# Two chunks of queries and probabilities turned by DMA under a rewritten instruction list, in a sorted-attention kernel with a cosine-gated layer behind it

## The chip, the cores and the metric

The kernel runs on one core of one Trainium2 chip. A core has a matrix engine (TensorE, "PE" in the profile, its weight loads "PEld"), a vector engine (VectorE, "DVE"), an engine for functions of one element (ScalarE, "ACT"), a general engine (GpSimd, "POOL") and SyncE ("SP"), which here does nothing but issue DMAs. Each engine works through its own instructions in order and waits on semaphores for the others. 16 DMA engines move data; GpSimd and SyncE each feed a queue of their own to them. The metric is device time in microseconds (us) of one execution, the median of several.

## The reference

Four batches of eight heads, 768 positions, 64 dimensions. The positions form eight blocks of 96. A softmax-like matrix P of 8 by 8 per head, normalised five times by rows and columns, mixes the blocks of keys and of values; each block of queries then attends to one mixed block. The result, 3072 tokens of 512, goes through a layer with a cosine gate.

```python
for _ in range(5):
    P = P - np.max(P, axis=-1, keepdims=True)
    P = np.exp(P)
    P = P / (np.sum(P, axis=-1, keepdims=True) + 1e-09)
    P = P / (np.sum(P, axis=-2, keepdims=True) + 1e-09)
k_sorted = np.einsum('bhij,bhjcd->bhicd', P, k_b).reshape(B, H, S, D)
v_sorted = np.einsum('bhij,bhjcd->bhicd', P, v_b).reshape(B, H, S, D)
scores = scale * np.matmul(q_b, k_sb.transpose(0, 1, 2, 4, 3))
scores = scores - np.max(scores, axis=-1, keepdims=True)
attn = np.exp(scores)
attn = attn / (np.sum(attn, axis=-1, keepdims=True) + 1e-09)
x = np.matmul(attn, v_sb)          # then heads side by side: 3072 x 512
h = x @ w_in
out = (h * np.cos(h)) @ w_out
```

## The kernel before

**Chunks and units.** The tokens are cut into eight chunks `n` of 384 (half a batch each), a chunk into four units `u` of one block. A unit needs its scores (queries against mixed keys, L438 or L745), the row maximum and its subtraction on DVE, the exponent on ACT (`expo`, L515), the probabilities turned (`pT`), the attention product (L570), its normalisation on DVE and that result turned again (`xT`). A chunk then goes up (`up`, L614; chunk 0 in quarters, `up_four`, L798), through sine with a shift on ACT and the gate on DVE, and down (`down`, L639; `down_four`, L819).

**Turning.** A tile is turned either by PE (a matmul with the identity, then a copy out of PSUM by ACT or DVE) or by a DMA transpose that SyncE issues. `expo(n, u, True)` leaves the probabilities to PE (`p_ps` and `p_ev`); without `True` it issues the DMA (L533), which reads one of three `p_buf` tiles in turn. Queries of chunks below `NQ = 3` are loaded by one DMA (L119) and turned by PE (`q_products`, L268, with `q_place_half`); later ones come by eight smaller DMAs (L129) between columns that `zeros_between` has cleared, and SyncE turns them (`q_transpose_dma`, L149). `q_turned` has two halves by the parity of the chunk, `q_mem` and part of `kbuf` hold the untransposed queries.

**Keys and values.** Batches 0 and 1 share one mixing matrix in the places where 128 rows are used, batches 2 and 3 (`g = 1`) another. Batch 0's keys are mixed by `kp` (L408), batch 1's by `ks`, those of batches 2 and 3 by `k_sort_g` from the tile `pair`. `k_swap` moves mixed keys between partition halves by two DMAs (L421, L422). Values arrive in `vbuf`; GpSimd's `v_permute` (L179) copies them to `vperm` in pieces of some value dimensions, and the value products (L726 for batch 0, L448 for batch 1, L458 for batches 2 and 3) read one dimension `d` each as a stationary tile. They take 128 columns from column `d * 96` on, of which 96 belong to `d` and 32 to the next dimension, so the last product of a piece also reads the start of the next piece.

**Order.** There is no scheduler: the order of the calls in the program is the order on every engine. Up to chunk 1's start the list is written out call by call, with extra matmuls on a zero tile (`keep_warm`, the argument `fill`) in places; from `up(1, 0)` on it is in loops with slots. A tile taken from a pool (`big` has three buffers in PSUM, `acc` two) waits until the tile that held the buffer before has been read. GpSimd's queue is also a list: its loads go out between its copies and fills, and a `hold` (a copy of one element, L541, or L426 for `hold_keys`) keeps what is behind it back until a DMA has landed. A load of GpSimd's also waits until the eighth one before it has landed.

Of the kernel before, what the change touches and what calls it, by code (L numbers as in the profile page):

```python
# [18 lines left out]
def kernel(  # L19
# [15 lines left out]
    nc = tc.nc  # L35
# [131 lines left out]
    VQ = 16  # L167
# [58 lines left out]
    def ones(g):  # L226
        nc.gpsimd.memset(vS[g][:, :, D:D + 1], 1.0)
# [196 lines left out]
    def hold_keys():  # L424

        nc.gpsimd.tensor_copy(held[:], kT[1][:, 1, 0, :1])  # L426

    def keys_of(n, u, h2, hp):
        g, b2, ih = where(n)
        z = slice(hp, hp + 2)  # L430
# [7 lines left out]
        nc.tensor.matmul(  # L438
            out, q_of(n, hp)[:, x:x + 128], keys_of(n, u, h2, hp), start=True, stop=True)
# [14 lines left out]

    def v_sort_g(d0, nd, eng, pool, tag):
        ps = pool.tile([128, nd, 4 * NB], FP32, name="vs", tag=tag)
        for t in range(nd):
            nc.tensor.matmul(  # L458
                ps[:, t], v_cols(d0 + t, True), bds[1].rearrange("p x i -> p (x i)"),
                start=True, stop=True)  # L460
        copy_on(eng, vS[1][:, :, d0:d0 + nd], ps[:blk].rearrange("p t n -> p n t"))

# [47 lines left out]
    def expo(n, u, on_pe=False):  # L510
        p = p_bufs[cnt[0] % NP]
        cnt[0] += 1


        nc.scalar.activation(  # L515
            p[:, :, :blk], s_t.pop((n, u)).rearrange("p e h c -> p (e h) c"), AF.Exp,
            scale=scale)
        if u == 0 and n in (NQ, NQ + 1):

            w = 2 * H2 * blk  # L520
            c = 2 * (QZ + D) + (n - NQ) * w
# [197 lines left out]
    def v0(z, pool, tag, fill=0):  # L719
        o = ps["v", z] = pool.tile([128, 8, 2 * NB], FP32, name="vs", tag=tag)  # L720
        keep_warm(fill, o.rearrange("p t n -> p (t n)"))
        for t in range(8):

            d = z * 8 + t
            w = 1 if d >= VN else min(8 - t, 2)
            nc.tensor.matmul(  # L726
                o[:, t:t + w].rearrange("p w n -> p (w n)"), v_cols(d, d >= VN),
                bdv[:, :H].rearrange("p x i -> p (x i)").unsqueeze(1).to_broadcast(
                    [128, w, 2 * NB]), start=True, stop=True)

# [111 lines left out]
        v_sort_g(next(wz), 8, eng, *B)  # L842
        next(wz)

    kp(2, *B)
    kp(0, *B)
# [4 lines left out]
    k_place(2, A, 1)  # L851
    k_place(2, V, 0)
    kp(1, *B)
    k_place(0, A, 0)
    blocks.append(block([pick[:, :, z * PB:(z + 1) * PB] for z in (1, 0)]))
    k_place(1, V, 0)
    k_place(1, A, 1)
    values_matrix()
    k_place(0, A, 1)
    s_ps(0, 0, fill=3)  # L860
    v0(4, *C)
    s_max(0, 0)
    v0(0, *B)
    v0e(4, A)
    s_sub(0, 0)
    s_ps(0, 3)
    v0e(0, A)
    v0(5, *C)
    s_max(0, 3)
    load_w_out(0)  # L870
    v0e(5, A)
    s_ps(0, 1)
    load_w_out(1)
    load_w_out(2)
    load_w_out(3)
    v0(6, *C)
    ones(0)
    expo(0, 0, True)
    s_ps(0, 2)
    s_sub(0, 3)  # L880
    v0(1, *C)
    v0e(6, A)
    s_max(0, 1)
    expo(0, 3, True)
    v0(3, *B, fill=2)
    s_sub(0, 1)
    v0e(1, A)
    p_ps(0, 0, *C, fill=2)
    v0e(3, A)
    s_max(0, 2)  # L890
    v0(7, *C)
    expo(0, 1, True)
    kxp(2)
    v0(2, *B, fill=1)
    p_ev(0, 0, V)
    v0e(7, A)
    s_sub(0, 2)
    kxp(0)
    p_ps(0, 1, *C)
    v0e(2, A)  # L900
    p_ps(0, 3, *C)
    p_ev(0, 1, V)
    expo(0, 2, True)
    kxp(1)
    av_products(0, 0)
    z_turned(1)
    av_norm(0, 0, True)
    av_products(0, 1)
    p_ev(0, 3, A)
    p_ps(0, 2, *C)  # L910
    av_norm(0, 1, True)
    x_ps(0, 0, *B)
    load(kbuf, 0, kin_d[1])
    p_ev(0, 2, A)
    load(vbuf, 64, vin_d[1])
    picks(pick_pair, (2, 3))
    av_products(0, 3, fill=2)
    av_norm(0, 3, True)
    x_ps(0, 1, *C)
    x_ev(0, 0, A)  # L920
    av_products(0, 2)
    q_products(1, 0, 0, 16, *C)
    x_ev(0, 1, A)
    av_norm(0, 2, True)
    x_ps(0, 3, *B)
    q_place_half(1, 0, 1, A)
    up_four(0, 0, 0)
    z_vperm()
    up_four(0, 0, 1)
    x_ev(0, 3, V)  # L930
    q_place_half(1, 0, 0, V)
    up_four(0, 3, 0)
    up_four(0, 3, 1)
    z_turned(0)
    cos_four(0, 0)
    p_pads()
    up_four(0, 1, 0)
    cos_four(0, 3)
    gate_four(0, 0)
    x_ps(0, 2, *C)  # L940
    up_four(0, 1, 1)
    gate_four(0, 3)
    up_four(0, 2, 0)
    cos_four(0, 1)
    up_four(0, 2, 1)
    x_ev(0, 2, V)
    gate_four(0, 1)
    up_four(1, 2, 0)
    cos_four(0, 2)
    up_four(1, 2, 1)  # L950
    gate_four(0, 2)
    up_four(1, 1, 0)
    cos_four(1, 2)
    up_four(1, 1, 1)
    gate_four(1, 2)
    up_four(1, 3, 0)
    cos_four(1, 1)
    up_four(1, 3, 1)
    gate_four(1, 1)
    q_products(1, 1, 0, 16, *C)  # L960
    cos_four(1, 3)
    last = block([pick_pair[:]], *C)
    q_place_half(1, 1, 0, V)
    up_four(1, 0, 0)
    q_place_half(1, 1, 1, A)
    gate_four(1, 3)
    up_four(1, 0, 1)
    s_ps(1, 1)
    spread(bds[1], last)
    cos_four(1, 0)  # L970
    s_ps(1, 0)
    s_max(1, 1)
    down_four(0, 0)
    gate_four(1, 0)
    load_q(2)
    down_four(0, 1)
    load_pair(pair, kin_d, 0 * CD // 2, 1 * CD // 2)
    load_pair(pair, kin_d, 1 * CD // 2, 2 * CD // 2)
    v_permute(slice(64, 128))
    down_four(0, 2)  # L980
    s_sub(1, 1)
    down_four(1, 0)
    s_max(1, 0)
    expo(1, 1, True)
    ks(5, *B)
    s_ps(1, 3)
    s_sub(1, 0)
    kse(5, A)
    down_four(0, 3)
    s_max(1, 3)  # L990
    expo(1, 0, True)
    ks(4, *B)
    s_ps(1, 2)
    down_four(1, 1)
    down_out(0, A)
    s_max(1, 2)
    kse(4, A)
    p_ps(1, 1, *C)
    s_sub(1, 3)
    down_four(1, 2)  # L1000
    p_ev(1, 1, A)
    down_four(1, 3)
    s_sub(1, 2)
    expo(1, 3, True)
    p_ps(1, 0, *B)
    down_out(1, A)
    av_products(1, 1)
    p_ps(1, 3, *B)
    p_ev(1, 0, A)
    av_norm(1, 1, True)  # L1010
    down_four(2, 0)
    expo(1, 2, True)
    p_ev(1, 3, V)
    av_products(1, 0)
    x_ps(1, 1, *B)
    down_four(2, 1)
    av_norm(1, 0, True)
    x_ev(1, 1, A)
    p_ps(1, 2, *B)
    av_products(1, 3)  # L1020
    p_ev(1, 2, A)
    down_four(2, 2)
    av_norm(1, 3, True)
# [179 lines left out]
```

## Time and profile before

| | us |
|---|---|
| median of 3 executions | 235.54 (234.93 to 236.42) |
| profiled execution, its own time | 235.54 |
| its span in the profile | 233.6 |
| PE busy | 224.1 |
| DVE busy | 171.0 |
| ACT busy | 154.4 |
| GpSimd busy | 95.9 |

Times in the profile count from the start of the span, to which the time of an execution adds 1.9 us around it. A row of a timeline reads: start, duration, engine, line of the program, operation, written tile and read tiles, how many instructions were merged; in brackets how long the engine stood idle before and who released it. A duration of PE includes the way through the array, so the distance from one group's start to the next is what a group costs. A row of a stretch ("66.00:70.00") gives its length, the busy time of PE, PEld, DVE, ACT and POOL with their numbers of instructions, PE's granted clock, the share of the 16 DMA engines (several packets at once can take it over 1) and GB/s.

### The profile page before, as it was taken

Reading aid. Unit: us, or ns where it says so; the run is one execution under the profiler, and the core shown is the slowest. Engines: PE = TensorE matmul, PEld = TensorE weight load, DVE = VectorE, ACT = ScalarE, POOL = GpSimd, SP = SyncE. Lnnn points to the kernel's source line nnn. Section 1 sums busy time; section 2 is a strip of 40 time slices with the busy share of each in tenths; the row PEclk is TensorE's granted clock in tenths of the full one; section 3 lists DMA queues with packets and bytes.
Section 4 is the critical chain, followed back from the end, with each engine's and each line's share of the span. In section 5 each row is a group of like instructions: output and inputs, shape, how many; then the busy total and the mean of one; then the engine's idle time right before and its main releaser. Section 6 shows DMA issues by size and latency. Waiting matters only on the chain.

```text
span 233.6 us, 5420 instructions
## 1 busy us (share of the span) xinstructions
PE 224.1 (96%) x2212; PEld 141.8 (61%) x2212; DVE 171.0 (73%) x291; ACT 154.4 (66%) x209; POOL 95.9 (41%) x121
## 2 busy tenths in 40 slices
PE   8778999999999999998999999999999999999994
PEld 3367899567665656655666546655665566556553
DVE  6769867987789867885498885997699769745700
ACT  5648886776889758795788565655665566816621
POOL 7999999399950093992609002600000000000000
PEclk9999999999999999999999999999999999999999
DMA  5999999993999799898999679934933360351012
GB/s 73 227 190 206 203 206 227 204 223 124 124 134 175 123 166 151 130 198 134 139 145 101 96 99 195 170 65 88 177 128 64 73 186 0 68 144 45 3 45 90
DMA packets 67672, 31.19 MB, mean 134 GB/s; under 512 B 56384, under 2 KB 63168, under 8 KB 67392
## 3 DMA queue, kind: packets, MB, share of 16 engines
q0 software_dynamic: 24048, 13.64, 43.3%
q1 hardware_dynamic: 43312, 17.02, 35.1%
q8 instruction: 17, 0.28, 0.5%
q10 hardware_dynamic: 288, 0.20, 0.3%
q14 instruction: 7, 0.06, 0.1%
HBM read 27.27 MB, written 6.29 MB: 144 GB/s over the span
## 4 chain that ended last, share of the span: by engine, by line
PE 82%; DMA 8%; DVE 3%; POOL 3%; ACT 1%; issue 1%; SPq 0%; ACTq 0%; DVEq 0%; POOLq 0%
PE h L614 30%; PE o L639 27%; DMA kv<-in_v_dram 5%; PE h L798 5%; PE o L819 4%; PE sc L438 4%; PE av L570 3%; POOL vperm L179 3%; DMA pT<-p_buf 2%; PE ks L408 2%; PE o L1167 2%; DMA kTs<-kTs 1%; DVE xn L583 1%; PE vs L458 1%; PE pps L776 1%
## 5 line engine op out<-in xcount | busy, mean ns | idle before, releaser
L614 PE MATMUL h<-xT,w_in_t 128*128 128x384 bf16 x448 | 78.4, 326 | 0.0
L639 PE MATMUL o<-w_out_t,gg 128*128 128x512 bf16 x320 | 76.3, 379 | 0.0
L622 DVE TENSOR_TENSOR gg<-c,h 128x768 bf16<-128x768 f32 x56 | 52.7, 949 | 19.5 <-ACT c L618 19.4
L618 ACT ACTIVATE c<-h,half_pi 128x768 f32<-128x768 f32 x56 | 50.4, 900 | 24.5 <-PE h L614 23.6
L614 PEld LDWEIGHTS <-w_in_t 128*128 128x128 bf16 x448 | 42.2, 98 | 26.3 <-DVE xT L259 0.3
L639 PEld LDWEIGHTS <-gg 128*128 128x128 bf16 x320 | 29.1, 99 | 27.8
L515 ACT ACTIVATE p_buf<-s 96x768 bf16<-96x768 f32 x32 | 26.7, 842 | 5.6 <-DVE s L489 4.7
L179 POOL COPY vperm<-kv 64x768 bf16<-64x768 bf16 (+2 forms) x12 | 28.4, 2408 | 4.4 <-DMA kv<-in_v_dram 4.4
L489 DVE TENSOR_TENSOR s<-sc,mx 96x384 f32<-96x384 f32 (+1 forms) x33 | 24.3, 736 | 1.6
L487 DVE TENSOR_REDUCE mx<-sc 96x4 f32<-96x384 f32 (+1 forms) x33 | 24.0, 728 | 0.0
L583 DVE TENSOR_TENSOR xn<-av,r 96x512 bf16<-96x512 f32 x32 | 22.0, 687 | 1.1
L129 POOL DMA_DIRECT2D kv<-in_q_dram x24 | 16.0, 677 | 0.8 <-issue 0.5
L438 PE MATMUL sc<-kTs,q_turned 128*128 128x96 bf16 x224 | 15.4, 206 | 0.3 <-DMA kTs<-kTs 0.3
L257 ACT CAST kTs<-ks 128x512 bf16<-128x512 f32 x20 | 11.3, 582 | 6.3 <-PE ks L408 5.3
L581 DVE RECIPROCAL r<-av 96x8 f32<-96x8 f32 x32 | 6.4, 199 | 12.0 <-PE av L570 11.8
L438 PEld LDWEIGHTS <-q_turned 128*128 128x128 bf16 x224 | 12.6, 98 | 4.0 <-DVE s L489 0.6
L257 ACT COPY kv<-o 128x512 f32<-128x512 f32 (+2 forms) x10 | 5.2, 523 | 14.1 <-PE o L639 11.5
L129 POOL DMA_DIRECT2D q_mem<-in_q_dram x16 | 10.7, 690 | 4.6 <-DMA kv<-in_v_dram 4.2
L819 PE MATMUL o<-w_out_t,gg 128*128 128x512 bf16 x48 | 11.7, 379 | 0.0
L259 DVE COPY kv<-o 128x512 f32<-128x512 f32 (+1 forms) x5 | 3.1, 611 | 11.1 <-PE o L1167 8.5
L798 PE MATMUL h<-xT,w_in_t 128*128 128x192 bf16 x128 | 11.1, 246 | 0.0
L798 PEld LDWEIGHTS <-w_in_t 128*128 128x128 bf16 x128 | 10.5, 98 | 0.0
(128 smaller groups left out, 276.9 us busy)
## 6 DMA issues: line engine op xcount, KB each, us to landing
out_dram<-kv SPq DMA_DIRECT2D x12, 256.0 KB, 2.6
out_dram<-o_s SPq DMA_DIRECT2D x10, 256.0 KB, 3.7
w_in_t<-in_moe_w_in_dram POOLq DMA_DIRECT2D x4, 512.0 KB, 11.6
w_out_t<-in_moe_w_out_dram POOLq DMA_DIRECT2D x4, 512.0 KB, 12.6
kv<-in_k_dram POOLq DMA_DIRECT2D x2, 768.0 KB, 10.0
kv<-in_v_dram POOLq DMA_DIRECT2D x2, 768.0 KB, 13.3
pair<-in_k_dram POOLq DMA_DIRECT2D x2, 768.0 KB, 12.3
kv<-in_v_dram POOLq DMA_DIRECT2D x6, 256.0 KB, 5.6
```

The source lines that it names most:

```text
L129: nc.gpsimd.dma_start(out=q_heads[:, i, :, e], in_=src[:, ih * IC + i, :, e])
L179: nc.gpsimd.tensor_copy(dst, src)
L438: nc.tensor.matmul(out, q_of(n, hp)[:, x:x + 128], keys_of(n, u, h2, hp), start=True, stop=True)
L487: nc.vector.reduce_max(mx[:], scv, axis=AX.X)
L489: nc.vector.tensor_tensor(s, scv, mx.to_broadcast(list(s.shape)), op=ALU.subtract)
L515: nc.scalar.activation(p[:, :, :blk], s_t.pop((n, u)).rearrange("p e h c -> p (e h) c"), AF.Exp, scale=scale)
L583: nc.vector.tensor_tensor(xn.rearrange("p h e d -> p e h d"), avv[:, :, :, :D], r.to_broadcast([blk, 2, H2, D]), op=ALU.mult)
L614: nc.tensor.matmul(h[:, f2, :w], w_in_t[:, kk, f * 128:(f + 1) * 128], xT[n][:, kk], start=(kk == 0), stop=(kk == KC - 1))
L618: nc.scalar.activation(c[:], h[:, :, :w], AF.Sin, bias=half_pi[:, 0:1])
L622: nc.vector.tensor_tensor(gt[n, fp // 2][:, f:f + 2], c[:], h[:, :, :w], op=ALU.mult)
L639: nc.tensor.matmul(o[:], gt[n, f // 4][:, f % 4, ts * 128:(ts + 1) * 128], w_out_t[:, f, :], start=(f == 0), stop=(f == FC - 1))
L798: nc.tensor.matmul(o[:, part, f2 * w:(f2 + 1) * w], w_in_t[:, kk, f * 128:(f + 1) * 128], xT[0][:, kk, h * w:(h + 1) * w], start=(kk == 0) ...
```

## The change

Five things are changed.

1. `NQ` is 2. Chunk 2's queries are no longer loaded by one DMA and turned by 32 transposes of PE and four copies of DVE: `q_mem` is cleared between the heads (`zeros_between(2)`), eight DMAs fill it, and SyncE turns it with two DMA transposes. The fills of `q_turned[0]` (`z_turned(0)`) and the second clearing of `q_mem` before chunk 4 go. Unit 0 of chunks 3 and 4 keeps its place in `kbuf`.
2. Units 1 and 0 of chunk 1 are turned by a DMA transpose (`expo(1, 1)` and `expo(1, 0)` without `True`); eight transposes of PE and a copy go for each.
3. The keys of batches 2 and 3 come to `pair` in four pieces in place of two halves: the last piece before the queries, the other three between GpSimd's copies of batch 1's values.
4. `hold_keys` goes, and the first three of the six value loads of batches 2 and 3, which stood behind it, join the other three. All six now stand behind chunk 4's query loads.
5. The last value product of each block of products takes 96 columns, and writes 96 rows, in place of 128.

The list up to `up(1, 0)` is written anew around this: value and key products, exponents and evictions of chunk 0 in another order and on other engines, the quarters of `up_four` and `down_four` in another order (the down projection of chunk 0's first 128 tokens last), `k_swap` ahead of the last pieces, twelve fills in place of ten.

```diff
-    QR, NQ = 4, 3
+    QR, NQ = 4, 2
...
-    def v_cols(d, permuted):
-        return vperm[:, d * blk:d * blk + 128] if permuted else vv[:, d]
+    def v_cols(d, permuted, m=128):
+        return vperm[:, d * blk:d * blk + m] if permuted else vv[:, d]
...
+            m = 128 if t < nd - 1 else blk
             nc.tensor.matmul(
-                ps[:, t], v_cols(d0 + t, b == 1 or d0 + t >= D // 2)[rows],
+                ps[:m, t], v_cols(d0 + t, b == 1 or d0 + t >= D // 2, m)[rows],
...
+    load_pair(pair, kin_d, 3 * CD // 4, 4 * CD // 4)
+    load_q(2)
...
+    for z in range(4):
+        if z < 3:
+            load_pair(pair, kin_d, z * CD // 4, (z + 1) * CD // 4)
+        v_permute(slice(64, 128), z * VQ, hi=(z + 1) * VQ)
...
-    expo(1, 1, True)
+    expo(1, 1)
...
+    q_transpose_dma(2)
...
-    hold_keys()
-    load_pair(vbuf, vin_d, 0 * CD // 6, 1 * CD // 6)
-    load_pair(vbuf, vin_d, 1 * CD // 6, 2 * CD // 6)
-    load_pair(vbuf, vin_d, 2 * CD // 6, 3 * CD // 6)
...
-    for z in range(3, 6):
+    load_q(4)
+    for z in range(6):
         load_pair(vbuf, vin_d, z * CD // 6, (z + 1) * CD // 6)
-    load_q(4)
```

On GpSimd, from the clearing of `p_buf`'s last tile to the copies of batch 1's values, there stood before (a line, an operation, written and read tile, the shape, how often):

```order
L685 MEMSET p_buf_109 96x8x32
L119 DMA q_mem<-in_q_dram 96x8x256
L92 DMA pair<-in_k_dram 128x3072 x2
L179 COPY vperm<-kv 64x1536 x4
L137 MEMSET kv 96x16x64 x2
```

and at the same place now:

```order
L683 MEMSET p_buf_109 96x8x32
L137 MEMSET q_mem 96x16x64 x2
L92 DMA pair<-in_k_dram 128x1536
L129 DMA q_mem<-in_q_dram 96x4x64 x8
L92 DMA pair<-in_k_dram 128x1536
L179 COPY vperm<-kv 64x1536
L92 DMA pair<-in_k_dram 128x1536
L179 COPY vperm<-kv 64x1536
L92 DMA pair<-in_k_dram 128x1536
L179 COPY vperm<-kv 64x1536 x2
L137 MEMSET kv 96x16x64 x2
```

The one query load has become two fills and eight loads, and the copies alternate with key loads.

Further on GpSimd, from chunk 3's query loads to the copies of the values of batches 2 and 3 (`-` before, `+` now):

```order
 L129 DMA kv<-in_q_dram 96x4x64 x8
-L426 CAST held<-kTs 128x1
-L92 DMA kv<-in_v_dram 128x1024 x3
-L137 MEMSET q_mem 96x16x64 x2
-L541 CAST held<-pT 96x1
-L92 DMA kv<-in_v_dram 128x1024 x3
+L539 CAST held<-pT 96x1
 L129 DMA q_mem<-in_q_dram 96x4x64 x8
+L92 DMA kv<-in_v_dram 128x1024 x6
 L179 COPY vperm<-kv 128x1536 x4
```

All value loads have moved behind the hold on unit (2, 2)'s probabilities and behind chunk 4's queries.

In SyncE's queue, from the load of the mixing weights to the transposes of chunk 3's queries (`q_turned_94` is the half for even chunks, `q_turned_95` the one for odd ones):

```order
 L81 DMA P<-in_sort_net_dram 32x64
-L629 DMA out_dram<-o_s 128x512 x2
-L629 DMA out_dram<-c 128x512
+L531 DMA_TRANSPOSE pT<-p_buf_108 128x8x96
+L627 DMA out_dram<-o_s 128x512
+L531 DMA_TRANSPOSE pT<-p_buf_107 128x8x96
+L149 DMA_TRANSPOSE q_turned_94<-q_mem 128x16x96 x2
+L627 DMA out_dram<-c 128x512
 L421 DMA kTs<-kTs 64x1536
 L422 DMA kTs<-kTs 64x1536
+L627 DMA out_dram<-o_s 128x512
 L149 DMA_TRANSPOSE q_turned_95<-kv 128x16x96 x2
```

Two transposes of probabilities and two of queries now stand ahead of the swap of keys, and one output store behind it.

More of the change, by code (lines that the diff above doesn't have):

```diff
@@ L843, in w_two @@
         next(wz)
-    kp(2, *B)
-    kp(0, *B)
+    kp(2, *B, fill=1)
+    blocks.append(block([pick[:, :, z * PB:(z + 1) * PB] for z in (1, 0)]))
     v_permute(slice(0, 64), 32, False, 8, 40)
@@ L850 @@
     v_permute(slice(0, 64), 56, False, 8, 64)
-    k_place(2, A, 1)
-    k_place(2, V, 0)
+    k_place(2, A, 0)
+    k_place(2, V, 1)
     kp(1, *B)
+    values_matrix()
+    kp(0, *B)
+    k_place(1, V, 0)
+    v0(0, *C)
     k_place(0, A, 0)
[L855 to L858, printed above, removed]
+    k_place(1, V, 1)
+    s_ps(0, 0)
+    v0e(0, A)
+    s_max(0, 0)
+    v0(4, *C, fill=1)
     k_place(0, A, 1)
-    s_ps(0, 0, fill=3)
@@ L861 @@
-    v0(4, *C)
-    s_max(0, 0)
-    v0(0, *B)
+    v0(5, *C)
     v0e(4, A)
+    s_ps(0, 3)
     s_sub(0, 0)
[L866 to L869, printed above, removed]
+    v0e(5, A)
+    v0(2, *C)
     load_w_out(0)
-    v0e(5, A)
-    s_ps(0, 1)
     load_w_out(1)
     load_w_out(2)
+    s_max(0, 3)
     load_w_out(3)
+    expo(0, 0, True)
+    ones(0)
     v0(6, *C)
-    ones(0)
-    expo(0, 0, True)
-    s_ps(0, 2)
+    v0e(2, A)
     s_sub(0, 3)
-    v0(1, *C)
-    v0e(6, A)
-    s_max(0, 1)
@@ L906 @@
+    v0(3, *C, fill=1)
+    s_sub(0, 1)
+    v0e(7, A)
+    s_ps(0, 2, fill=1)
+    v0e(3, A)
+    p_ev(0, 0, V)
+    v0(1, *C)
+    kxp(0)
+    expo(0, 1, True)
+    s_max(0, 2)
+    v0e(1, A)
+    p_ps(0, 1, *B, fill=2)
+    kxp(1)
+    s_sub(0, 2)
+    p_ev(0, 1, A)
+    av_products(0, 0, fill=1)
+    kxp(2)
     z_turned(1)
     av_norm(0, 0, True)
+    p_ps(0, 3, *C, fill=3)
+    expo(0, 2, True)
     av_products(0, 1)
-    p_ev(0, 3, A)
-    p_ps(0, 2, *C)
     av_norm(0, 1, True)
     x_ps(0, 0, *B)
+    p_ev(0, 3, A)
@@ L940 @@
-    x_ps(0, 2, *C)
+    x_ev(0, 2, V)
     up_four(0, 1, 1)
     gate_four(0, 3)
-    up_four(0, 2, 0)
+    up_four(1, 3, 0)
     cos_four(0, 1)
-    up_four(0, 2, 1)
-    x_ev(0, 2, V)
+    up_four(1, 3, 1)
     gate_four(0, 1)
+    up_four(1, 1, 0)
+    cos_four(1, 3)
+    up_four(1, 1, 1)
+    gate_four(1, 3)
+    up_four(1, 0, 0)
+    cos_four(1, 1)
+    up_four(1, 0, 1)
+    gate_four(1, 1)
+    q_products(1, 0, 0, 16, *C)
+    zeros_between(2)
+    cos_four(1, 0)
+    load_pair(pair, kin_d, 3 * CD // 4, 4 * CD // 4)
@@ L948 @@
+    load_q(2)
+    last = block([pick_pair[:]], *C)
+    q_place_half(1, 0, 0, V)
     up_four(1, 2, 0)
-    cos_four(0, 2)
+    q_place_half(1, 0, 1, A)
+    gate_four(1, 0)
     up_four(1, 2, 1)
[L951 to L963, printed above, removed]
@@ new lines @@
+    s_sub(1, 1)
+    down_four(1, 2)
+    s_max(1, 2)
+    expo(1, 1)
+    ks(5, *B)
+    s_ps(1, 0)
+    s_sub(1, 2)
+    kse(5, A)
+    down_four(1, 3)
+    s_max(1, 0)
+    expo(1, 2, True)
+    ks(2, *B)
+    s_ps(1, 3)
+    down_four(2, 1)
+    kse(2, A)
+    s_sub(1, 0)
+    down_out(1, A)
+    down_four(2, 2)
+    s_max(1, 3)
+    expo(1, 0)
+    ks(4, *B)
+    p_ps(1, 2, *B)
+    s_sub(1, 3)
+    kse(4, A)
+    down_four(2, 3)
+    q_transpose_dma(2)
+    p_ev(1, 2, V)
+    expo(1, 3, True)
@@ L976 @@
+    ks(1, *B)
+    ks(3, *C)
+    kse(1, V)
+    av_products(1, 1)
+    down_out(2, A)
+    p_ps(1, 3, *B)
+    av_norm(1, 1, True)
+    av_products(1, 2)
+    p_ev(1, 3, A)
+    down_four(0, 0)
+    av_norm(1, 2, True)
+    kse(3, A)
+    av_products(1, 3)
+    av_products(1, 0)
+    av_norm(1, 0, True)
+    x_ps(1, 2, *B)
     down_four(0, 1)
-    load_pair(pair, kin_d, 0 * CD // 2, 1 * CD // 2)
-    load_pair(pair, kin_d, 1 * CD // 2, 2 * CD // 2)
-    v_permute(slice(64, 128))
+    x_ev(1, 2, A)
```

155 lines of the change are left out of this document (47 added, 108 removed).

## The prediction, made before the changed kernel ran

> **What bounds the kernel now.** I read the page's busy shares and its chain first, then TensorE's (PE's) waits, then the timelines of PE, GpSimd (POOL) and SyncE's queue (SPq) around the places that the new list rewrites. Busy time and share of each engine, and the chain's shares by engine:
>
> ```profile
> PE 224.1 (96%) x2212; PEld 141.8 (61%) x2212; DVE 171.0 (73%) x291; ACT 154.4 (66%) x209; POOL 95.9 (41%) x121
> ```
>
> ```profile
> PE 82%; DMA 8%; DVE 3%; POOL 3%; ACT 1%; issue 1%; SPq 0%; ACTq 0%; DVEq 0%; POOLq 0%
> ```
>
> PE's waits that matter here (total, times, longest):
>
> ```profile
> PE av L570 <- DMA pT<-p_buf: 0.6, 1, 0.6
> ...
> PE sc L438 <- DMA kTs<-kTs: 0.3, 1, 0.3
> ```
>
> PE is busy 224.1 of 233.6 us and carries 82% of the chain; after the start it waits 0.6 us for one DMA transpose of probabilities and 0.3 us for one key swap. So a microsecond of PE work that goes is a microsecond won, and whatever PE newly waits for is lost whole: nothing behind it makes a wait good.
>
> **What leaves PE.** Chunk 2's queries were 32 transposes, each of the two units of chunk 1 was 8 (PE's timeline; then the chain in order of time):
>
> ```profile
> 56.59 0.90 PE L268 MATMUL qps<-ident,q_mem 96*64 96x96 bf16 x32
> 57.42 1.47 PE L614 MATMUL h<-xT,w_in_t 128*128 128x384 bf16 x8
> ```
>
> ```profile
> 49.46 0.36 PE pps L776 x8
> ```
>
> The queries take 57.42 − 56.59 = 0.83 us, a unit 0.36. Gone: 0.83 + 2 × 0.36 = **−1.55**. Their copies on DVE and ACT go too, but PE waited for neither: nothing.
>
> **The start.** GpSimd's four value copies, and two rows of PE:
>
> ```profile
> 14.13 5.83 POOL L179 COPY vperm<-kv 64x768 bf16<-64x768 bf16 x4 [0.41 <-DMA kv<-in_v_dram]
> ```
>
> ```profile
> 20.02 0.20 PE L726 MATMUL vs<-bdv,vperm 128*128 128x64 bf16 x1 [0.62 <-POOL vperm L179]
> ...
> 28.57 2.64 PE L798 MATMUL h<-xT,w_in_t 128*128 128x192 bf16 x30
> ```
>
> The copies end at 14.13 + 5.83 = 19.96. The product that waits for the last (the last row of the third of four value products, since its 128 columns reach into the next piece) starts at 20.02, and the first up projection 8.55 us after that. With 96 columns each value product goes with its own piece: the four become possible at about 15.6, 17.1, 18.5 and 20.0, and more of the other work fits in between. Behind the last of them stand, before the first up projection, two value products straight from kv, four groups of p transposes, one score group, four attention products, two x transposes, 16 query transposes and nine fills, which I count at 6.7 to 7.2 us from such groups. So it starts near 27.2: **−1.4**. Bounds: 0 if the copies between those groups come late, −1.8 if none does. Inside the up projections stands one x transpose more than before, +0.17.
>
> **Narrow products.** Weight loads by shape (busy, mean ns):
>
> ```profile
> L570 PEld LDWEIGHTS <-pT 96*128 96x128 bf16 x126 | 5.6, 97 | 2.6 <-DMA pT<-p_buf 1.0 <-ACT pT L257 0.3
> ...
> L570 PEld LDWEIGHTS <-pT 96*96 96x96 bf16 x18 | 2.2, 122 | 0.0
> ```
>
> 96 columns took 122 ns, 128 columns 97. The list has 23 narrow value products, at most 23 × 25 ns = 0.6 us, partly under the matmul beside it: +0.3 (0 to +0.6).
>
> **Two units of chunk 1 by DMA.** Unit 1's exponent, and a quarter of a down projection in the chain:
>
> ```profile
> 43.46 0.84 ACT L515 ACTIVATE p_buf<-s 96x768 bf16<-96x768 f32 x1 [0.80 <-DVE s L766]
> ```
>
> ```profile
> 45.07 0.86 PE o L819 x4
> ```
>
> It ended at 44.3 and now ends about a microsecond earlier, 43.5. Up to its attention product stand four score groups, eight down quarters (0.86 each), five key groups and one group of p transposes: PE wants it near 49, after 5.5 us. Unit 0 is tighter: going through the list its exponent ends 4 us later, at 47.5, and its product is wanted at 51.2, after 3.7. What a transpose may take there: the stretch 44 to 52 (the last columns are clock, share of the DMA engines, GB/s), then medians from issue to landing of the run's transposes, of the one that was issued into running value loads, and of two output stores between 44 and 56:
>
> ```profile
> 44.00:52.00 8.00, 8.00 (x101) 5.22 (x100) 6.50 (x11) 6.42 (x11) 6.96 (x3) 1.00 1.12 222
> ```
>
> ```profile
> pT<-p_buf SPq DMA_TRANSPOSE x9, 3.2
> ```
>
> ```profile
> kv<-p_buf SPq DMA_TRANSPOSE x1, 9.3
> ```
>
> ```profile
> out_dram<-o_s SPq DMA_DIRECT2D x2, 256.0 KB, 6.8
> ```
>
> The 16 DMA engines are full there (1.12), and in the new list the same loads run (keys in four pieces, queries in eight smaller loads). If a transpose lands in L, both units together lose L − 3.7, since PE's wait for the first is time for the second: 0 at 3.2, 3.1 at 6.8, 5.6 at 9.3. I take the 6.8, the only row of SyncE's queue in this stretch: **+3.1** (0 to +5.6). The Trainium skill (DMA: Bandwidth & Descriptors, Queues, rings and completion order) says that each DMA engine takes turns between its queues packet by packet; by that a transpose would need about twice its free 3.2, 6.4 us, a cost of 2.7. The 9.3 disagrees: more than a fair turn was lost there.
>
> **GpSimd up to chunk 3's queries.**
>
> ```profile
> 45.04 11.26 POOL L179 COPY vperm<-kv 64x1536 bf16<-64x1536 bf16 x4 [3.97 <-DMA kv<-in_v_dram]
> 56.54 1.83 POOL L137 MEMSET kv<- 96x1024 bf16 x2 [0.25 <-POOL vperm L179]
> 58.33 5.36 POOL L129 DMA_DIRECT2D kv<-in_q_dram  x8
> ```
>
> Chunk 2's one load becomes two fills (1.83 by the second row) and eight issues (5.36 by the third). Most of it runs in the 3.97 us in which GpSimd waited for values; 3 us of fills of q_turned go. The last of the eight issues goes out only after key piece 3 has landed, so the copies start near 48, with three key issues between them, and chunk 3's queries go out about 4 us later (62.4 to 67.7). Behind them in SyncE's queue stand the transposes of chunk 3's queries and then chunk 2's probabilities, wanted past 75: covered, 0 (to +2 if the waits above cost nothing, since PE is then 2 us earlier). Chunk 2's keys are swapped 2 us earlier against PE, so that wait goes: **−0.28**.
>
> **The value loads of batches 2 and 3.** Three of six pieces went out near 64; now all six are behind the hold on unit (2, 2) and behind chunk 4's eight query loads. GpSimd, then PE, then SyncE's queue:
>
> ```profile
> 81.23 0.18 POOL L541 CAST held<-pT 96x1 f32<-96x1 bf16 x1 [13.88 <-DMA pT<-p_buf]
> 81.68 1.60 POOL L92 DMA_DIRECT2D kv<-in_v_dram  x3 [0.27 <-issue]
> ...
> 92.88 11.27 POOL L179 COPY vperm<-kv 128x1536 bf16<-128x1536 bf16 x4
> ```
>
> ```profile
> 100.86 0.61 PE L458 MATMUL vs<-bd,vperm 128*128 128x128 bf16 x8
> ...
> 107.01 0.43 PE L570 MATMUL av<-vS,pT 96*128 96x65 bf16 x8 [0.60 <-DMA pT<-p_buf]
> ```
>
> ```profile
> 94.42 3.58 SPq L149 DMA_TRANSPOSE q_turned<-q_mem  x2
> ```
>
> Two stretches in which the DMA engines had only value loads, and only query transposes; then the landing of the value loads of 63 to 72 (shortest, median, longest):
>
> ```profile
> 66.00:70.00 4.00, 4.00 (x50) 2.65 (x47) 3.56 (x6) 3.43 (x5) 1.35 (x2) 1.00 1.02 150
> ```
>
> ```profile
> 71.00:73.50 2.50, 2.50 (x19) 1.32 (x18) 2.10 (x4) 2.47 (x3) 0.00 (x0) 1.00 1.22 258
> ```
>
> ```profile
> DMA to landing us min/median/max: 4.3/5.7/6.7
> ```
>
> PE paces both the hold and the value sort, so their distance stays, and I count in the times of before. There the copies began at 92.88 and the first quarter (11.27/4 = 2.82) was ready at 95.7, 5.2 us before 100.86. Now: hold until 81.4, gap 0.27, eight query issues 5.36: the first value load goes out at 87.05. Six of 256 KB take 10.5 us at 150 GB/s; the shortest landing, 4.3, is 1.75 of data and 2.5 around it. All have landed at 87.05 + 2.5 + 10.5 = 100.05, the first quarter is copied at 102.9, and PE stands 2.0 us. That is the lower end, since the engines were full at that rate. Chunk 4's query transposes, which went out at 94.42 after the loads, are now ready near 89 and fall among them: 0.79 MB at 258 GB/s, 3 us. I take **+4.8**; a 256 KB store on top gives 6.6. The stop covers the wait of 0.60 at 107.01: **−0.60**. GpSimd's later work moves with PE.
>
> **Sum.** −1.55 − 1.4 + 0.17 + 0.3 + 3.1 − 0.28 + 4.8 − 0.60 = +4.5. The profiled execution took 235.54 (a span of 233.6 and 1.9 around it), which is also the median of three (234.93 to 236.42): **240.0**.
>
> **Rivals.** *The loads land in time (faster).* Place: the first value sort of batches 2 and 3. The stretch 44 to 52 moved 222 GB/s; if six queued value loads reach that, they take 7.1 us, land at 96.6, and the first quarter is there at 99.4. It decides at a landing of 98.0. If chunk 1's transposes land within 3.7 too, −1.55 − 1.4 + 0.17 + 0.3 − 0.28 remain: 232.8. Against it: 150 GB/s was measured for just these loads. Chance 0.17.
>
> *Only the lower ends.* Transposes in time, value loads 2.0 late, the wait of 0.60 covered: 235.54 − 3.36 + 2.0 = 234.2, and up to 237.3 with the transposes at 6.8. Chance 0.22.
>
> *PE slows after its stop.* Its fills at the start:
>
> ```profile
> 1.00 5.34 PE L246 MATMUL idle<-warm 128*128 128x512 bf16 x14 [1.00 <-DVE warm L231]
> ...
> 7.65 1.04 PE L246 MATMUL idle<-warm 128*128 128x512 bf16 x4
> ...
> 9.93 0.61 PE L246 MATMUL idle<-warm 128*128 128x512 bf16 x2
> ```
>
> Taking the pair off, the first twelve ran at (5.34 − 0.61)/12 = 394 ns, two later ones at (1.04 − 0.61)/2 = 215. A stop long enough to bring the first state back costs 12 × 179 ns = 2.1 us: 242.1. After its start PE's longest wait for data it lacks is the 0.6 above, so no row shows from which length that happens. The Trainium skill (TensorE: Matmul & The Clock Gate, The HAM clock gate) halves the clock after some 3.4 us of idleness; by that a stop of 4.8 does it. Chance 0.16.
>
> *Forecast*, both waits and no slower clock, 238 to 241.5: 0.45.
>
> **Numbers.** A measurement of this kernel tells 1% (2.4 us) from no change. Faster (below 233.2): the first rival, 0.17. Within 1%: most of the second, 0.20. Slower: 0.63. The range leaves out the first rival and little above: from 233.5 to 243.5, the slower clock with the value loads at 6.2.
>
> **What would show it.** In the new profile: a wait of 2 to 7 us for GpSimd's vperm copies at the first value sort of batches 2 and 3 (line 456 there); waits for DMA pT<-p_buf at the attention products of chunk 1 (line 568), 3 us together; the first up projection near 27.2. No wait at line 456 makes the forecast wrong by its largest term, landings under 4 us near 48 by its second. A granted clock below 1.00 behind the stop speaks for the third rival.

## The result, and the profile after

| | before, us | changed, us | ratio, 95% interval |
|---|---|---|---|
| first measurement, median | 235.24 (234.75 to 236.42) | 243.8 (241.39 to 248.63) | 1.0272 [1.0224, 1.0319] |
| second measurement, median | 235.11 (234.63 to 237.05) | 246.9 (244.79 to 251.77) | 1.0474 [1.0404, 1.0545] |

The change makes the kernel 2.7 to 4.7% slower by two ratios whose intervals do not meet, and its executions lie further apart than those of before. Each ratio leaves out executions over 1.5% above the fastest of the same kernel, which are two of the first four and one of the second four, and the first profile's (248.63, span 246.5) is among them. The rows below are therefore from the second measurement, whose profiled execution took 245.7 with a span of 243.6; the first profile has its largest waits at the same places (7.8 us at the key swap, where the second has 6.2). Line numbers are those of the changed kernel (L434 was L438, L568 was L570, L456 was L458, L612 was L614).

The page's busy times, and the clock in 40 slices of 6.1 us:

```profile
PE 227.0 (93%) x2166; PEld 142.1 (58%) x2166; DVE 169.7 (70%) x289; ACT 152.9 (63%) x206; POOL 98.1 (40%) x125
...
PEclk9999999989959999999999999999999999999999
```

TensorE (PE) has 46 matmuls fewer and yet 2.9 us more busy time: twice its clock fell. Its waits:

```profile
PE sc L434 <- DMA kTs<-kTs: 6.2, 1, 6.2
PE av L568 <- DMA pT<-p_buf: 1.4, 2, 1.2
...
PE pps L775 <- ACT p_buf L513: 0.5, 1, 0.5
```

The key swap, 0.3 us before, is now the largest wait of the kernel. PE's timeline at the places the prediction spoke of:

```profile
27.96 0.83 PE L797 MATMUL h<-xT,w_in_t 128*128 128x192 bf16 x8
...
39.77 0.84 PE L434 MATMUL sc<-kTs,q_turned 128*128 128x96 bf16 x16
...
50.93 0.43 PE L568 MATMUL av<-vS,pT 96*128 96x65 bf16 x8 [1.19 <-DMA pT<-p_buf]
51.87 0.56 PE L775 MATMUL pps<-ident,p_buf 96*96 96x96 bf16 x8 [0.50 <-ACT p_buf L513]
...
59.03 1.46 PE L612 MATMUL h<-xT,w_in_t 128*128 128x384 bf16 x8
...
68.75 0.48 PE L434 MATMUL sc<-kTs,q_turned 128*128 128x96 bf16 x4 [6.21 <-DMA kTs<-kTs]
69.03 2.76 PE L612 MATMUL h<-xT,w_in_t 128*128 128x384 bf16 x8
...
74.00 0.34 PE L434 MATMUL sc<-kTs,q_turned 128*128 128x96 bf16 x4
...
110.84 0.62 PE L456 MATMUL vs<-bd,vperm 128*128 128x128 bf16 x8 [0.18 <-POOL vperm L179]
...
236.59 3.70 PE L1159 MATMUL o<-w_out_t,gg 128*128 128x256 bf16 x48
```

The same places in PE's timeline of before, as far as the prediction did not show them:

```profile
40.20 0.84 PE L438 MATMUL sc<-kTs,q_turned 128*128 128x96 bf16 x16
...
61.17 0.33 PE L438 MATMUL sc<-kTs,q_turned 128*128 128x96 bf16 x4 [0.28 <-DMA kTs<-kTs]
...
64.41 0.34 PE L438 MATMUL sc<-kTs,q_turned 128*128 128x96 bf16 x4
...
226.65 3.70 PE L1167 MATMUL o<-w_out_t,gg 128*128 128x256 bf16 x48
```

Taking one from the other gives the whole account:

| PE reaches | before | changed | later by | what came in between |
|---|---|---|---|---|
| chunk 1's first scores | 40.20 | 39.77 | -0.43 | the earlier start |
| chunk 1's up projection | 57.42 | 59.03 | +1.61 | waits 1.19 + 0.50, half clock, less PE work |
| chunk 2's first scores | 61.17 | 68.75 | +7.58 | the key swap's wait |
| chunk 2's next scores | 64.41 | 74.00 | +9.59 | half clock |
| the value sort of batches 2 and 3 | 100.86 | 110.84 | +9.98 | the late value loads, 0.18 |
| the last products | 226.65 | 236.59 | +9.94 | nothing |

Of the 10.0 us by which the spans differ, 8.0 arise between 57 and 74 us, at the swap: 6.0 of waiting and 2.0 of slow clock behind it. The granted clock by stretches (columns as in the prediction):

```profile
52.50:55.50 3.00, 3.00 (x30) 1.88 (x27) 0.92 (x3) 1.24 (x2) 3.00 (x3) 0.50 1.12 185
...
62.50:66.00 3.50, 0.04 (x1) 0.00 (x0) 0.00 (x0) 0.00 (x0) 3.50 (x6) 1.00 1.12 72
66.00:66.50 0.50, 0.00 (x0) 0.00 (x0) 0.00 (x0) 0.00 (x0) 0.50 (x2) 0.56 1.01 393
66.50:72.50 6.00, 3.75 (x22) 2.23 (x23) 2.06 (x3) 2.04 (x3) 0.91 (x2) 0.50 1.39 158
```

PE stands still from 62.5 on; its clock halves 3.5 us later and stays at half until past 72.5, so what it has to do from 68.75 until then takes about twice as long (an up projection 2.76 us at 69.03, against 1.46 at 59.03). The other half-clocked stretch, 3 us, follows the two short waits of chunk 1.

Now the DMAs that went out between 43 and 62 us: their number, size, and median time from issue to landing, in the changed kernel:

```profile
pair<-in_k_dram POOLq DMA_DIRECT2D x3, 384.0 KB, 6.3
...
kTs<-kTs SPq DMA_DIRECT2D x2, 192.0 KB, 10.0
...
pT<-p_buf SPq DMA_TRANSPOSE x2, 6.9
q_turned<-q_mem SPq DMA_TRANSPOSE x2, 9.5
```

and before, of the same view:

```profile
kTs<-kTs SPq DMA_DIRECT2D x2, 192.0 KB, 2.9
```

SyncE's queue in the changed kernel:

```profile
51.22 5.83 SPq L149 DMA_TRANSPOSE q_turned<-q_mem  x2
...
57.93 0.54 SPq L421 DMA_DIRECT2D kTs<-kTs  x1
```

The swap itself was issued early enough: at 57.93, 4.6 us before PE stood ready at 62.5 (68.75 - 6.21). But it landed after 10.0 us instead of 2.9. It was not alone in that: the second query transpose, issued at 53.9 and ahead of it in the queue, landed after 12.4 us, at 66.3, and the last key piece, issued at 54.12, after 10.2, where the two before it took 6.3 and 5.4. The question for the experiments is what slowed it, and what each part of the change costs without it.

### The profile page after: what moved, and what is told of

It reads as the page before. It is cut to its first block, busy times and chain, and to the rows that moved or that the text cites. A ratio compares the mean times of both kernels' runs of the same rounds, so it can differ in the third digit from the quotient of the medians.

```text
span 246.5 us, 5349 instructions
## 1 busy us (share of the span) xinstructions
PE 227.8 (92%) x2166; PEld 142.3 (58%) x2166; DVE 169.6 (69%) x289; ACT 153.0 (62%) x206; POOL 98.0 (40%) x125
## 4 chain that ended last, share of the span: by engine, by line
PE 69%; DMA 17%; DVE 7%; ACT 2%; POOL 2%; issue 1%; SPq 0%; DVEq 0%; ACTq 0%; POOLq 0%
PE h L612 29%; PE o L637 22%; DMA q_mem<-in_q_dram 6%; DMA pT<-p_buf 5%; PE h L797 4%; DMA kTs<-kTs 4%; PE sc L434 3%; PE av L568 3%; DMA xT<-xn 2%; PE o L1159 1%; PE ks L408 1%; DVE xn L581 1%; PE o L818 1%; POOL w_in_t L160 1%; DVE mx L485 1%
## 5 line engine op out<-in xcount | busy, mean ns | idle before, releaser
L612 PE MATMUL h<-xT,w_in_t 128*128 128x384 bf16 x448 | 80.9, 333 | 0.3 <-DMA xT<-xn 0.3
L612 PEld LDWEIGHTS <-w_in_t 128*128 128x128 bf16 x448 | 42.9, 100 | 28.4 <-issue 3.1
L179 POOL COPY vperm<-kv 64x768 bf16<-64x768 bf16 (+2 forms) x12 | 28.2, 2388 | 10.5 <-DMA kv<-in_v_dram 10.4
L434 PE MATMUL sc<-kTs,q_turned 128*128 128x96 bf16 x224 | 15.6, 208 | 7.8 <-DMA kTs<-kTs 7.8
L434 PEld LDWEIGHTS <-q_turned 128*128 128x128 bf16 x224 | 12.7, 98 | 11.5 <-issue 7.8
L129 POOL DMA_DIRECT2D q_mem<-in_q_dram x24 | 15.9, 675 | 2.1 <-DMA pair<-in_k_dram 1.0
L797 PEld LDWEIGHTS <-w_in_t 128*128 128x128 bf16 x128 | 10.4, 98 | 0.0
```

What stands on the lines that cost most here:

```text
L129: nc.gpsimd.dma_start(out=q_heads[:, i, :, e], in_=src[:, ih * IC + i, :, e])
L179: nc.gpsimd.tensor_copy(dst, src)
L434: nc.tensor.matmul(out, q_of(n, hp)[:, x:x + 128], keys_of(n, u, h2, hp), start=True, stop=True)
L612: nc.tensor.matmul(h[:, f2, :w], w_in_t[:, kk, f * 128:(f + 1) * 128], xT[n][:, kk], start=(kk == 0), stop=(kk == KC - 1))
L797: nc.tensor.matmul(o[:, part, f2 * w:(f2 + 1) * w], w_in_t[:, kk, f * 128:(f + 1) * 128], xT[0][:, kk, h * w:(h + 1) * w], start=(kk == 0) ...
```

## The experiments

Each run is compared with the kernel before on the same chip (medians 235.07 to 235.63). The changed kernel itself was run again as a base:

> The changed kernel once more, unchanged, on the chip of the next three. All theories: about 241 to 243 us. If its profile is of a shorter execution than the first (span 246.5), the wait for the key swap before chunk 2's first scores should be shorter than the 7.8 us there, and the time at half clock too; the attention products of chunk 1 should still wait 1 to 2 us for their DMA transposes.

That is the second measurement above: 246.9, ratio 1.0474 [1.0404, 1.0545], more than the 241 to 243 expected. The wait at the swap is shorter than in the first profile (6.2 against 7.8), as expected of a shorter execution.

**Part 1 undone: chunk 2's queries by PE.**

```diff
-    QR, NQ = 4, 2
+    QR, NQ = 4, 3
...
-    q_transpose_dma(2)
...
+    q_transpose(2, 0, (V, V), *C)
+    q_transpose(2, 1, (V, V), *B)
```

> The changed kernel with chunk 2's queries loaded in one piece and turned by PE again (part 1 undone; PE has 0.83 us more work). Theory K (the query transposes stand ahead of the key swap in SyncE's queue, run into the key loads of GpSimd's queue, and hold the swap back; PE then waits and drops to half clock): the wait before chunk 2's first scores falls under 1 us, no half clock behind it, 236 to 238 us. Theory V of the forecast (the late value loads cost most): within 1 us of the changed kernel. Theory P (the two transposes of probabilities cost most): also within 1 us of it.

Measured: 246.75 (241.48 to 248.29, too far apart for a ratio), where theory K expected 236 to 238. The profile is of the longest execution, so its rows count only together with the later run without part 3. The wait at the swap is gone, but PE's timeline has new ones ahead of it:

```profile
52.74 0.43 PE L568 MATMUL av<-vS,pT 96*128 96x65 bf16 x8 [3.11 <-DMA pT<-p_buf]
...
59.63 0.65 PE L568 MATMUL av<-vS,pT 96*128 96x65 bf16 x8 [3.28 <-DMA pT<-p_buf]
```

Its landings between 43 and 62 us:

```profile
pair<-in_k_dram POOLq DMA_DIRECT2D x2, 384.0 KB, 11.3
...
pT<-p_buf SPq DMA_TRANSPOSE x2, 10.5
```

Without the query transposes the two probability transposes take 10.5 us, and the key pieces beside them 11.3. So the collision with the key loads does not need the query transposes. Of the swap this run says nothing: PE's new waits made its keys late, and it went out at 63.85, when the last key piece (issued at 51.20, 10.8 us to landing) was in.

**Part 2 undone: units 1 and 0 of chunk 1 by PE.**

```diff
-    expo(1, 1)
+    expo(1, 1, True)
...
-    expo(1, 0)
+    expo(1, 0, True)
...
+    p_ps(1, 1, *B)
...
+    p_ev(1, 1, A)
```

> The changed kernel with units 1 and 0 of chunk 1 turned by PE again (part 2 undone; PE has 0.72 us more work). Theory P: 237 us or less. Theory K: the waits for pT (1.7 us) and the first stretch of half clock go, but PE only comes earlier to the key swap, so the time stays within 1.5 us of the changed kernel and the wait before chunk 2's first scores stays over 4 us. Theory V: within 1.5 us of the changed kernel.

Measured: 246.62 (246.32 to 248.37), 1.0509 [1.0457, 1.0562]: nothing gained over the changed kernel, as theories K and V expected. The waits of chunk 1 and the half clock behind them are gone, the swap still takes 10.9 us to land and PE waits 7.3 for it. What part 2 costs in chunk 1 is hidden by the wait that follows.

**The key loads moved away.** Three of the four key pieces behind chunk 3's queries and a hold on the swapped keys; the transposes stay.

```diff
-        if z < 3:
-            load_pair(pair, kin_d, z * CD // 4, (z + 1) * CD // 4)
...
     load_q(3)
+    hold_keys()
+    for z in range(3):
+        load_pair(pair, kin_d, z * CD // 4, (z + 1) * CD // 4)
```

> The changed kernel with the key pieces 0 to 2 issued behind chunk 3's query loads and a hold on the swapped keys, so that nothing of GpSimd's queue runs beside chunk 2's query transposes. Theory K in its full form (collision with the key loads is what slows the transposes): each of the two query transposes lands in 3 to 5 us, the swap in 3 to 5 us, PE waits under 1.5 us before chunk 2's first scores, 236 to 238 us. If the order in SyncE's queue alone does it, collision or not: the wait stays over 3 us, and the time over 239.

Measured: 240.47 (239.07 to 241.93), 1.0231 [1.0171, 1.0291], 6.4 us less than the changed kernel, but 2.5 above theory K's 236 to 238. Landings between 43 and 62 us:

```profile
kTs<-kTs SPq DMA_DIRECT2D x2, 192.0 KB, 2.9
...
pT<-p_buf SPq DMA_TRANSPOSE x2, 6.1
q_turned<-q_mem SPq DMA_TRANSPOSE x2, 4.3
```

The swap lands in 2.9 us again and PE doesn't wait for it. The probability transposes stay at 6.1, so their lateness does not need these key pieces (the last two of chunk 2's query loads went out beside them, at 45.32 and 46.83), and the waits of chunk 1 remain (1.39 and 0.50). And PE, now in time, meets the next wait, the one forecast as the lower end:

```profile
105.23 0.62 PE L460 MATMUL vs<-bd,vperm 128*128 128x128 bf16 x8 [2.31 <-POOL vperm L179]
```

**Parts 1 and 2 undone together** (the edits of the two runs above).

> The changed kernel with parts 1 and 2 undone: chunk 2's queries and units 1 and 0 of chunk 1 turned by PE; the rewritten list, the keys in four pieces, the late value loads and the narrow products stay. Theory C (DMA transposes beside GpSimd's key loads slow both down; nothing else in this stretch costs): no wait over 0.5 us at the key swap of chunk 2 and at chunk 1's attention products, clock 1.00 up to the value sort of batches 2 and 3; there the late loads cost 2 to 2.5 us and about 1.7 us of half clock behind it, since PE now comes in time; 237 to 239 us. Rival R (the rewritten list loses by itself, by its order of evictions and its key pieces between the copies): waits of 3 us or more remain before 75 us of the span, 241 us or more.

Measured: 237.4 (236.93 to 239.63), 1.0078 [1.0046, 1.0109]. The key pieces stand in the list where the changed kernel has them, now with no transposes beside them:

```profile
pair<-in_k_dram POOLq DMA_DIRECT2D x2, 384.0 KB, 5.3
...
kTs<-kTs SPq DMA_DIRECT2D x2, 192.0 KB, 2.9
```

Together with the runs above: transposes without key pieces 2.9 us for the swap, key pieces without transposes 2.9, both 10.0, and 10.9 with part 2 undone. Neither alone slowed the swap. One reservation: in the run with both parts undone the three pieces went out 2 to 6 us earlier than in the changed kernel (the last at 52.06, landing at 58.0), and the swap only met the end of the last one, for 1.2 us. The value sort waits 1.4 us, not 2 to 2.5, and the clock stays at 1.00 behind it.

**Key loads later and part 2 undone.**

> The run with the key loads behind chunk 3's queries, and in it units 1 and 0 of chunk 1 by PE as well: of the change by DMA only chunk 2's queries are left. Theory P2 (in that run the 1.4 and 0.5 us of waits at chunk 1's attention products, with the half clock behind them, are what is left of part 2): -1.9 of waits, -1.7 of clock, +0.7 of PE work, from 240.5 to about 237.5, with the wait of 2.3 us at the value sort still there. Rival (the waits only move): 239.5 to 241.

Measured: 243.45 (242.47 to 244.41), 1.0323 [1.0271, 1.0374], 6 us more than expected and 3.0 more than with part 2 in place (2.2 by the ratios, whose intervals just overlap). The waits of chunk 1 go, but PE comes earlier to chunk 2's first attention product (at 77.14, with part 2 in place at 79.05):

```profile
81.18 0.43 PE L572 MATMUL av<-vS,pT 96*128 96x65 bf16 x8 [4.04 <-DMA pT<-p_buf]
```

Landings between 66 and 82 us:

```profile
pair<-in_k_dram POOLq DMA_DIRECT2D x3, 384.0 KB, 8.6
...
q_turned<-kv SPq DMA_TRANSPOSE x2, 7.5
```

The key pieces, moved, run beside chunk 3's query transposes, and chunk 2's probabilities are queued behind these on SyncE: they went out from 78.08 on, with part 2 in place from 76.61. The collision was moved, not removed.

**Part 4 undone as well: the value loads as before.** What is left is the list, the key pieces and the narrow products.

```diff
     load_q(3)
+    hold_keys()
+    for z in range(3):
+        load_pair(vbuf, vin_d, z * CD // 6, (z + 1) * CD // 6)
...
-    load_q(4)
-    for z in range(6):
+    for z in range(3, 6):
         load_pair(vbuf, vin_d, z * CD // 6, (z + 1) * CD // 6)
+    load_q(4)
```

> The kernel with parts 1 and 2 undone, and part 4 undone too: three of six value loads of batches 2 and 3 early, behind the hold on the keys, the others ahead of chunk 4's queries. Left are the list, the keys in four pieces and the narrow products. Theory V (the late value loads cost 2 to 2.5 us and a half clock of 1.7 us): 4 us less than with both by PE, no wait over 0.3 us at the value sort, 233.5 to 235 us, the same as or up to 0.6% faster than before. Rival: the loads cost less than 1 us; within 1 us of the other.

Measured: 235.73 (234.99 to 236.69), 1.0001 [0.997, 1.0033]. Undoing part 4 brings 0.8% (1.0078 against 1.0001), 1.8 us where 4 were expected. And the list brings nothing: PE reaches chunk 1's first scores 0.50 us earlier than before, but chunk 1's up projection, with nearly the same work ahead of it, 0.55 later:

```profile
39.70 0.84 PE L438 MATMUL sc<-kTs,q_turned 128*128 128x96 bf16 x16
...
57.97 1.47 PE L616 MATMUL h<-xT,w_in_t 128*128 128x384 bf16 x8
```

**Part 4 alone, in the kernel before.**

```diff
-    hold_keys()
-    load_pair(vbuf, vin_d, 0 * CD // 6, 1 * CD // 6)
...
-    for z in range(3, 6):
+    load_q(4)
+    for z in range(6):
         load_pair(vbuf, vin_d, z * CD // 6, (z + 1) * CD // 6)
-    load_q(4)
```

> The kernel before with part 4 alone: all six value loads behind the hold on unit (2, 2) and chunk 4's query loads. The forecast's term: a wait of 4.8 us at the first value sort of batches 2 and 3, less 0.6 covered, 239.3 us; its lower end 2.0, 236.5 us, and 238.2 with a half clock of 1.7 us behind it. Theory V: between 2.0 and 2.5 us, half clock for some 3.4 us, 237.5 to 238.5. Rival (the loads land in time): 235.

Measured: 238.61 (237.43 to 240.12), 1.0121 [1.006, 1.0183]: 2.8 us.

```profile
104.51 0.62 PE L458 MATMUL vs<-bd,vperm 128*128 128x128 bf16 x8 [2.11 <-POOL vperm L179]
104.97 2.84 PE L639 MATMUL o<-w_out_t,gg 128*128 128x512 bf16 x8
```

The wait is 2.11 in the profiled execution, the longest of the four, and near the forecast's lower end (2.0). The down projection behind it, eight matmuls in 2.84 us where before they took 1.89, shows the half clock. Over the four executions the mean clock was 0.986, 0.997, 0.999 and 0.991: a wait of this length doesn't cost the same in each.

**Part 3 alone undone: the keys in two halves ahead of the copies.**

```diff
-    load_pair(pair, kin_d, 3 * CD // 4, 4 * CD // 4)
     load_q(2)
     last = block([pick_pair[:]], *C)
+    load_pair(pair, kin_d, 0 * CD // 2, 1 * CD // 2)
+    load_pair(pair, kin_d, 1 * CD // 2, 2 * CD // 2)
```

> The changed kernel with part 3 alone undone: the keys of batches 2 and 3 in two halves behind chunk 2's queries and ahead of GpSimd's copies, as before. Theory C (what costs is that key loads run while SyncE's queue turns chunk 2's queries and swaps keys, in whatever pieces): the halves go out by about 48 and move until about 56, the transposes at 51 fall on them again; the key swap waits 4 to 8 us, 243 to 247 us. Rival S (the pieces between the copies stretch the loads out, and that is what costs): the halves are done ahead of the swap, its wait is under 1 us, and 240 to 241 us remain, as where the key loads came later.

Measured: 244.3 (242.41 to 245.28), 1.0369 [1.0316, 1.0421]. The time is that of theory C, the place is not: PE doesn't wait for the swap (2.8 us to landing) but for the second probability transpose, issued at 47.70 and awaited until 58.91.

```profile
58.91 0.65 PE L568 MATMUL av<-vS,pT 96*128 96x65 bf16 x8 [6.16 <-DMA pT<-p_buf]
```

So it is not the cutting into pieces. In these runs key loads beside transposes slowed whichever of SyncE's DMAs was then under way.

**Matmuls on the zero tile in the wait**, in the changed kernel:

```diff
     v_sort_b(1, 16, 8, A, *C)
+    idle(28)
     qk_half(2, 0, 0, *C)
```

> The changed kernel with 28 more matmuls on the zero tile in front of the first scores of chunk 2, where PE waits for the key swap (28 x 215 ns = 6.0 us at full clock); nothing else is moved. Theory H (PE's half clock follows from its idleness): the wait at the swap falls to under 2 us, no granted clock under 0.95 in the 12 us behind it, where before some 4 to 6 us of work ran at half clock: 2 to 3 us less than the changed kernel's 246.9, 244 to 245 us. Rival (the half clock comes from something else, such as the load of the DMA engines): the clock falls at the same place and the time stays within 1 us of 246.9.

Measured: 244.08 (243.05 to 245.02), 1.0368 [1.0321, 1.0415], against 1.0474 [1.0404, 1.0545] without them; the intervals touch. The profile is plainer:

```profile
62.87 6.26 PE L246 MATMUL idle<-warm 128*128 128x512 bf16 x27
68.97 0.33 PE L434 MATMUL sc<-kTs,q_turned 128*128 128x96 bf16 x4
69.14 1.46 PE L612 MATMUL h<-xT,w_in_t 128*128 128x384 bf16 x8
```

PE comes to chunk 2's first scores no earlier than in the changed kernel (68.97 against 68.75), but the same up projection that took 2.76 us takes 1.46, and the clock is 1.00 all the way from 60 to 80 us, also where the DMA engines are as full as they were at half clock (1.39):

```profile
64.00:68.00 4.00, 3.94 (x19) 1.82 (x19) 0.95 (x1) 1.18 (x2) 3.93 (x6) 1.00 1.39 149
68.00:72.00 4.00, 4.00 (x35) 2.38 (x33) 1.53 (x3) 1.36 (x2) 0.00 (x0) 1.00 0.80 92
```

The half clock behind the swap follows from PE standing still, not from the load of the DMA engines. The profile shows one thing more: with the same list up to the fills, the swap landed in 6.2 us here, in 10.0 and 10.5 in the two profiles of the changed kernel. So the collision does not cost the same in each execution, and most of the fills ran after the keys had arrived.

**Part 5 alone, in the kernel before**: the narrow last products.

```diff
-                ps[:, t], v_cols(d0 + t, b == 1 or d0 + t >= D // 2)[rows],
+                ps[:m, t], v_cols(d0 + t, b == 1 or d0 + t >= D // 2, m)[rows],
```

> The kernel before with part 5 alone: the last value product of each block 96 wide. The forecast's reading of the start (the products that wait for the next piece of the copies, 0.71 and 0.62 us) and its +0.3 for narrow weight loads: those waits go in part, -0.3 to -0.7 us, and +0.3 of loads: between 234.6 and 235.4 us, 0 to 0.3% faster than before. Rival (the start is set by the copies, and the narrow loads cost their 0.6): 0.2% slower.

Measured: 235.02 (234.17 to 236.13, 12 executions), 0.9983 [0.996, 1.0006]. The waits of 0.7 and 0.6 us for the next piece of the copies fall to 0.2 in all. It is the only version with a ratio below 1, and its interval still includes 1.

## Why the prediction came out as it did

Forecast were 240.0 us, slower with a chance of 0.63, and a range of 233.5 to 243.5. It is slower. The first measurement's ratio puts the changed kernel at 241.6 (235.24 x 1.0272), inside the range; that median (243.8) and the second (246.9) lie above it. The direction, and a size near the forecast, came out by luck: the loss has a cause that the sum did not have, while its largest term nearly vanished. Point by point:

**The key swap, "so that wait goes: -0.28".** This step failed. It argued from the time of issue alone, and there its direction was right: 4.6 us of room, against 3.4 before (57.48, where its first DMA went out, to 60.89). It took over the landing time of before, 2.9 us, for a DMA that now had query transposes ahead of it in its queue, the second of them still under way, and key loads in the other. Measured: 6.2 us of wait and 2.0 of half clock, 8 of the 10 us. The prediction weighed the key pieces only against chunk 1's probability transposes. Chunk 2's query transposes, new in SyncE's queue, have no term in the sum at all: "covered, 0 (to +2)" is said of chunk 3's.

**"Whatever PE newly waits for is lost whole".** This premise failed too. The long wait at the swap swallowed others: undoing part 2 took the waits of chunk 1 away and PE waited 7.3 us at the swap in place of 6.2, and behind the swap the late value loads cost 0.18.

**The value loads, "+4.8", and the wait of 0.60 that they cover.** Mis-sized. Alone in the kernel before they cost a wait of 2.11 and some half clock, 2.8 us in all; in the run with the key loads later 2.31; with parts 1 and 2 undone 1.4. The term's own parts, 2.0 and 3.05 (0.79 MB at 258 GB/s), make 5.0 and not 4.8. Of the 3 us for chunk 4's query transposes hardly any came: in the kernel with part 4 alone the copies began 19.2 us after the hold, where the lower end had counted 18.65 without these transposes. They were held up themselves: in SyncE's queue they took 12.2 us to issue, from 89.59 on. In the changed kernel only 0.18 was left. The premise "PE paces both the hold and the value sort, so their distance stays" failed there. GpSimd's timeline:

```profile
89.11 0.18 POOL L539 CAST held<-pT 96x1 f32<-96x1 bf16 x1 [21.70 <-DMA pT<-p_buf]
89.62 5.30 POOL L129 DMA_DIRECT2D q_mem<-in_q_dram  x8 [0.33 <-issue]
...
107.92 11.23 POOL L179 COPY vperm<-kv 128x1536 bf16<-128x1536 bf16 x4 [9.10 <-DMA kv<-in_v_dram]
```

From hold to value sort it is 110.84 - 89.11 = 21.7 us, before 100.86 - 81.23 = 19.6. The loads still took as long from the hold to the copies (18.8), so the longer distance swallowed the wait.

**Two units by DMA, "+3.1".** The landing was 6.9, taken as 6.8. The loss had another make-up: 1.19 us at the first unit and 0.50 behind it, then half clock for the 3 us that follow, worth about 1.5; the slower PE then came to the second unit when it had landed. Together about 3.2. But undoing this part gained nothing, since the swap's wait came next.

**The start, "-1.4".** Less than half of it was there: the up projections began at 27.96 instead of 28.57, and chunk 1's scores 0.43 earlier. The narrow products did take away the two waits at the copies, as the run with part 5 alone shows. But the last product on GpSimd's copies started at 20.34, not 20.0, and from there to the up projection it took 7.6 us, not 6.7 to 7.2; PE's rows have waits of 0.28 for ScalarE just ahead of it and 0.25 for DVE behind it. The -1.55 of PE work and the +0.3 of narrow loads could not be read off singly under the waits.

**The third rival, the slower clock.** It came, at +2.0 us (forecast 2.1), but behind the swap and not behind the value sort. There the Trainium skill (TensorE: Matmul & The Clock Gate, The HAM clock gate), with its 3.4 us of idleness, agrees with the trace: the clock halved 3.5 us after PE stopped. In chunk 1 the trace goes further than the page: 1.19 and 0.50 us with 0.4 us of work between them were enough.

**What stays open** is how the DMA engines come to lose so much. The Trainium skill (DMA: Bandwidth & Descriptors, Queues, rings and completion order) lets each DMA engine take turns between its queues, packet by packet. With two queues such turns would, by an estimate from that rule, double a transfer's time at most where the packets are alike. The two query transposes took 2.2 times as long in the median (9.5 against 4.3), near that, but the second of them 12.4. The swap's 3.4 times (10.0 against 2.9) also holds its wait behind that transpose. Which transfer holds up the other inside the engines no run here separates. Nor does one show why the swap's landing differs so much between executions of the same list (6.2 to 10.5).

## What to carry to other kernels

Price a DMA that is moved, or that others are moved ahead of, at the landing time it will have among its new neighbours in all queues, not at the one it had. Work taken off the bounding engine by DMA transposes was paid for here where bulk loads ran at the same time, and in a kernel whose DMA engines are full there may be no free place for either: moving one of the two shifted the collision to the next transfer that somebody waits for. And a wait on a matrix engine that is otherwise always busy can cost more than its length: ask what half clock it brings behind it (2.0 us behind the 6.2 here).

## What was not expected of the hardware

- DMA transposes from SyncE's queue and GpSimd's key loads (384 KB as written) slowed each other: query transposes 4.3 us without the key pieces and 9.5 beside them, key pieces 5.3 without the transposes and in most runs 6.3 to 11.3 beside them, a swap of 192 KB queued behind the transposes 2.9 and 10.0. The run with the fills, with the same list ahead of them, had 7.6, 5.5 and 6.2.
- The share of busy DMA engines says little of what they move: before, 222 GB/s at a share of 1.12 with the key loads under way (44 to 52 us); in the changed kernel 72 at 1.12 while PE stood at the swap (62.5 to 66.0), with chunk 3's query loads in flight as well.
- PE's clock halved after waits of only 1.19 and 0.50 us close together, and for some 3 us; after 6.2 us of standing still it was half for 6 us and more. A wait of 2.11 (part 4 alone) brought it on in the profiled execution, one of 1.35 (parts 1 and 2 undone) did not.
